# Attention, gated block and Fourier mixing with a channel MLP: the end of the mixing written as an order of jobs

## Chip, cores, metric

The kernel runs on one core of a Trainium2 chip. Times are microseconds of device time; 611.52 us is the median of three runs before (610.66 to 611.62). The engines are named as in the profile: PE is TensorE, DVE VectorE, ACT ScalarE, POOL GpSimd, SP the engine that issues most transfers. PEld is TensorE's loading of weights.

## What is computed

Attention under a mask of hashed buckets (2 batches, 8 heads, 768 positions, 64 per head), a gated block and then, on `x` of 2 x 768 x 512, the part that the change touches:

```python
def _moe2_ref(x, w_ch1, w_ch2) -> np.ndarray:
    X = np.fft.fft(x, axis=1)
    X = np.fft.fft(X, axis=2)
    mixed = np.real(X).astype(np.float32)
    u = x + mixed
    mu = np.mean(u, axis=-1, keepdims=True)
    var = np.mean((u - mu) ** 2, axis=-1, keepdims=True)
    un = (u - mu) / np.sqrt(var + 1e-06)
    ch = np.maximum(un @ w_ch1, 0.0) @ w_ch2
    return (u + ch).astype(np.float32)
```

## The kernel before

The order of all instructions is the order in which the program writes them; there is no scheduler. Each engine works through its own part of that order, and waits when an input or a tile isn't there yet.

**Mixing** (`mixing`). The Fourier transform is done by tables. The output of the gated block comes in 12 parts: batch, even or odd half, and row block `kt` of 128. For each part `own` (L1286) makes 12 matmuls; `fold` copies the result to `y` (ACT) and folds its columns (DVE, L1299); `turn` transposes the fold (PE, L1306), takes the high half on ACT (L1311) and the low half `ft` on DVE (L1312); `along_d` multiplies by the table along the columns (PE, L1321) and splits into `ah` and `al` (ACT L1326 or L1331, DVE L1327 or L1332). Odd parts with `kt` 0 have two folds, so a batch has seven alongs. `mixed` (L1350) transforms along the positions, `total` (DVE, L1356 to L1361) and `both` (POOL, L1371) add it up to `u`.

**Normalising.** For each pair of row blocks (t and t + 3 of six): `stats` (DVE, L1105 and L1106), `root` (ACT, L1110), `scale` (DVE, L1115 and L1116: `rstd` and `shift`), `normal` (ACT, L1120: `un`), `u_transpose` (PE, L1127) and `u_parts` (`bh` on ACT, L1134, `bl` on DVE, L1135).

**Channel MLP** (`channel`). Weights come as 64-bit numbers and are taken apart by `from64`: six steps s0 to s5 on DVE (L221, L229, L230, L234, L235, L243) and ACT (L225, L249). `first` (PE, L1625) multiplies `bh` and `bl` by a block of the first weights, `relu_high` (ACT) and `relu_low` (DVE, L1617) make `hid`, `second` (PE, L1676) multiplies that by the second weights into six accumulators, `flush` (DVE) adds them to `u`. Four blocks of batch 0 are done in this plain way. From then on 13 steps use seven products of sums of weights and tokens instead of eight; the sums (`combos`, DVE, L1501 to L1509) are made ahead, the snapshots (L1747 and L1750) and low halves after a product.

**What sets the order.** In the mixing a loop over `i` from 0 to 13 writes own, alongs, turns and fold of successive parts, with the normalising of batch 0 and the conversion of weight block 3 (`channel_steps(3)`, one or two of its steps for each `i` from 8 on) behind them; after the loop the mixing products of batch 1. In the channel stage `follow` reads 16 strings, `ORDERS`, in which each word is a job of several instructions: `I0a` is the first channel product of weight block 0 for the first half of the rows, `h0a` and `l0a` its relu halves, `S00` a second product, `c51` a step of a weight conversion.

Of the kernel before, what the change touches and what calls it, by code (L numbers as in the profile page):

```python
# [76 lines left out]
""",
    """
M1 A3 A5 A6 M2 A4 s0 F0 c11 F1 B0 h11 B2 B1 M6 l11 M5 B3 s1 B5 B6 F2 B4 s3 F3 W0 M7 W1 M3 F4 c22 W2 c12 F5 A0+
h12 M4 W3 h22 A1+ G0 l12 h21 G1 l22 l21 G2 A3+ G3 A5+ A2+ G4 G5 A4+ A6+  # L80
""",
    """
M1 B0 B2 B1 M2 s0 B3 F0 B5 B6 c11 F1 f0 h11 M6 f1 l11 M5 s1 B4 A0+ F2 s3 A2+ A1+ F3 f2 M7 f3 M3 c22 A3+ F4 A5+
A6+ c12 F5 f4 h12 M4 h22 f5 G0 l12 h21 l22 G1 l21 G2 B0+ A4+ B1+ G3 B2+ G4 G5 B3+
""",
    """
M1 B5 B6 B4 M2 W0 s0 F0 c11 F1 W1 h11 M6 l11 W2 M5 A0+ A2+ s1 F2 s3 W3 F3 A1+ M7 A3+ M3 A5+ c22 A4+ F4 c12 F5
B0+ h12 M4 B2+ h22 B1+ G0 l12 h21 l22 G1 l21 G2 B3+ G3 B5+ B4+ G4 G5
""",
    """  # L90
M1 M2 s0 F0 c11 F1 h11 f0 M6 l11 f1 M5 s1 F2 s3 F3 f2 M7 f3 M3 c22 F4 c12 F5 h12 f4 h22 M4 l12 f5 G0 h21 l22
G1 l21 G2 G3 G4 G5
""",
    """
M1 M2 s0 F0 c11 F1 h11 M6 l11 M5 s1 F2 s3 F3 M7 M3 c22 F4 c12 F5 h12 h22 M4 l12 l22 G0 h21 G1 l21 G2 G3 G4 G5
""",
    """
M1 M2 s0 F0 c11 F1 h11 f0 M6 l11 f1 M5 s1 F2 s3 F3 f2 M7 f3 M3 c22 F4 c12 F5 h12 f4 h22 M4 l12 f5 G0 h21 l22
G1 l21 G2 G3 G4 G5
# [73 lines left out]
def block_kernel(  # L173
# [24 lines left out]
    def from64(words_of, raw, dst, half=False, parts=P, spare=False):  # L198
# [28 lines left out]
        def s2():  # L227
            g = word("g")
            nc.vector.tensor_scalar(g, hi, 0x1FF, 15, op0=ALU.bitwise_and, op1=ALU.logical_shift_left)  # L229
            nc.vector.scalar_tensor_tensor(g, lo, 17, g, op0=ALU.logical_shift_right, op1=ALU.bitwise_or)  # L230

        def s3():
            a, e = word("a"), word("e")
            nc.vector.scalar_tensor_tensor(a, hi, -(2 ** 31), a, op0=ALU.bitwise_and, op1=ALU.bitwise_or)  # L234
            nc.vector.tensor_scalar(e, a, -(2 ** 23), None, op0=ALU.bitwise_and)  # L235
# [15 lines left out]
        return [s0, s1, s2, s3, s4, s5]  # L251
# [773 lines left out]
    rstd, wst, wraw, wnext = [], [], {}, []  # L1025
# [13 lines left out]
    def late_tiles():  # L1039
# [14 lines left out]
        wst.append(pool(ctx, "wst", 2, side="right"))  # L1054
# [29 lines left out]
    def channel_steps(k, spare=False, load=True):  # L1084

        if k >= 2 * NF:
            return [lambda: None] * 6
        i, f = ORDER[k]
        w = w2[f % 4] if i else w1[f % 5]
        st = []  # L1090

        def step(q):
            if not st:
                st.extend(from64(channel_words, wraw[k], lambda: w, spare=spare))
            st[q]()
            if q == 3 and load:
                channel_load(k + 2)

        return [lambda q=q: step(q) for q in range(6)] + [lambda: channel_load(k + 2)] * (not load)

    def stats(b, kt):

        for t in (kt, kt + 3):
            st = wst[0].tile([P, 6], F32, tag="st", name="st")
            nc.vector.bn_stats(st, u[b][:, t, :])  # L1105
            nc.vector.bn_aggr(mu[b][:, t, :], st)  # L1106
# [11 lines left out]
    def normal(b, kt):  # L1118
        for t in (kt, kt + 3):
            nc.scalar.activation(  # L1120
                un[b, t], u[b][:, t, :], AF.Identity, bias=rstd[1][:, b, t : t + 1], scale=rstd[0][:, b, t : t + 1]
            )
# [7 lines left out]
    def u_parts(t, pu):  # L1130
        ts_ = slice(t % 3 * P, (t % 3 + 1) * P)
        pv_ = pu.rearrange("p (c t) -> p c t", c=NC)
        hi, lo = bh[0, t // 3][:, :, ts_], bl[0, t // 3][:, :, ts_]
        nc.scalar.copy(hi, pv_)  # L1134
        nc.vector.tensor_tensor(lo, pv_, f32(hi), op=ALU.subtract)  # L1135

    def mixing(es):
        nonlocal pp
# [155 lines left out]
        def fold(b, s, kt, yp):  # L1294
            y = ys[b, s, kt] = m2.tile([P, DM], F32, tag="y", name="y", bufs=7)
            nc.scalar.copy(y, yp)
            for part in (s,) if s == 0 or kt else (0, 1):
# [18 lines left out]
        def along_d(b, s, kt, part):  # L1316
            fh, fl = turned[b, s, kt, part]
            ops = [(x[:, i, :], tab[:, part, w, i, :]) for x, w in ((fh, 0), (fh, 1), (fl, 0)) for i in range(2)]
            pa = psum()
            for n, (x, w) in enumerate(ops):  # L1320
                nc.tensor.matmul(pa[:, :NL], x, w, start=n == 0, stop=n == len(ops) - 1)  # L1321
            ah, al = sums[b]
            slot = kt if part == s else 3
            high, low = ah[:, part, slot, :], al[:, part, slot, :]
            if part:
                nc.scalar.copy(high, pa[:, :NL])  # L1326
                nc.vector.tensor_tensor(low, pa[:, :NL], f32(high), op=ALU.subtract)  # L1327
            else:

# [56 lines left out]
        for i in range(len(jobs) + 2):  # L1386
# [47 lines left out]
            elif i > 10:  # L1434
                if i == 11:
                    root(0, 2)
# [390 lines left out]
```

## Time and profile before

| | |
|---|---|
| median of the runs | 611.52 us |
| the profiled execution | 613.5 us |
| its span | 611.7 us |
| TensorE busy | 595.0 us, 97% of the span |
| VectorE busy | 537.4 us, 88% |
| ScalarE busy | 378.3 us, 62% |
| GpSimd busy | 228.9 us, 37% |
| mean granted clock of TensorE | 0.994 |

TensorE is busy nearly all the time, so the table alone says little on where time could be lost. The attention ends near 255 us, the gated block and the mixing reach to about 352, and the channel MLP fills the rest. The page's slices of the span show one dip of TensorE's clock, in the slice that begins at 336.

### The profile page before, as it was taken

What the parts mean: (1) busy time and instruction counts of PE and PEld (TensorE: products, weight loads), DVE (VectorE), ACT (ScalarE), POOL (GpSimd) and SP (SyncE); (2) the same over time, 40 slices, a digit from 0 to 9 for tenths busy, and PEclk for the clock granted to TensorE, in tenths of its full rate; (3) what the DMA queues carried; (4) which work ended last, traced back from release to release, by engine and by line L of the source; (5) the groups of instructions that cost most, each with busy time, mean ns of one, the idle gap of its engine ahead of it and who ended that gap; (6) DMA issues with size and microseconds to landing.
All of it is one profiled execution on the core that took longest, in us unless ns stands there. A gap on an engine that the chain in (4) does not pass through costs nothing.

```text
span 611.7 us, 10422 instructions
## 1 busy us (share of the span) xinstructions
PE 595.0 (97%) x3633; PEld 544.6 (89%) x3633; DVE 537.4 (88%) x1041; ACT 378.3 (62%) x747; POOL 228.9 (37%) x272
## 2 busy tenths in 40 slices
PE   8999999999999999999998899999999999999997
PEld 6889999999899989998897899988998899998886
DVE  5999999999899999799789799999999999996345
ACT  5998899998899887863626566344344443442221
POOL 7251488886888898793350230000000000000000
PEclk9999999999999999999999799999999999999999
DMA  5957585856665750162012112021222323220014
GB/s 136 216 134 162 144 189 146 186 147 147 163 163 145 199 134 16 40 238 98 5 65 61 43 35 70 1 70 45 93 70 70 103 70 103 70 71 0 1 40 167
DMA packets 54958, 62.03 MB, mean 101 GB/s; under 512 B 29184, under 2 KB 42664, under 8 KB 54650
## 3 DMA queue, kind: packets, MB, share of 16 engines
q1 hardware_dynamic: 54170, 57.81, 35.7%
q0 software_dynamic: 432, 3.55, 1.5%
q8 instruction: 29, 0.48, 0.3%
q14 instruction: 23, 0.19, 0.1%
q10 hardware_dynamic: 304, 0.01, 0.0%
HBM read 36.74 MB, written 3.19 MB: 65 GB/s over the span
## 4 chain that ended last, share of the span: by engine, by line
PE 68%; DVE 18%; DMA 4%; ACT 3%; issue 2%; SPq 2%; POOL 2%; POOLq 0%; DVEq 0%; ACTq 0%
PE acc L1676 20%; PE pf L1635 14%; PE sp L638 6%; PE op L697 6%; PE ptp L674 5%; DVE sd L649 4%; DVE ptl L686 4%; PE pf L1625 3%; PE ps L302 3%; PE ps L1286 3%; DMA qk<-ht 3%; PE ps L1350 2%; PE late L302 1%; DMA xs<-xc 1%; PE early L302 1%
## 5 line engine op out<-in xcount | busy, mean ns | idle before, releaser
L649 DVE TENSOR_SCALAR_CACHE_REDUCE sd<-sp 128x768 f32<-128x768 f32 x96 | 91.2, 951 | 7.8 <-PE sp L638 7.5
L686 DVE TENSOR_TENSOR ptl<-ptp,pth 128x768 fp32r<-128x768 f32 x96 | 91.5, 954 | 5.5 <-ACT pth L682 3.8
L638 PE MATMUL sp<-qk 128*128 128x512 f32 (+1 forms) x384 | 91.4, 360 | 4.4 <-DVE sd L649 3.0
L656 ACT ACTIVATE sd<-sd,nm 128x768 f32<-128x768 f32 x96 | 90.2, 939 | 1.5 <-DVE sd L649 1.5
L682 ACT CAST pth<-ptp 128x768 fp32r<-128x768 f32 x96 | 77.1, 803 | 18.0 <-PE ptp L774 9.1
L674 PE MATMUL ptp<-ident,sd 128*128 128x128 f32 x576 | 78.5, 272 | 0.2 <-ACT sd L656 0.2
L697 PE MATMUL op<-pth,v 128*128 128x256 f32 x288 | 74.0, 283 | 1.3 <-ACT xc L710 1.3
L697 PE MATMUL op<-ptl,v 128*128 128x256 f32 x288 | 73.8, 286 | 0.0
L638 PEld LDWEIGHTS sp<-qk 128*128 128x128 f32 x384 | 58.2, 189 | 14.1 <-DVE sd L649 7.2
L674 PEld LDWEIGHTS ptp<-ident,sd 128*128 128x128 f32 x576 | 65.8, 140 | 1.1 <-ACT sd L656 0.5
L1676 PE MATMUL acc<-vh,hid 128*128 128x512 f32 x192 | 64.0, 391 | 0.0
L697 PEld LDWEIGHTS op<-pth,v 128*128 128x128 f32 x288 | 54.2, 188 | 6.3 <-ACT xc L710 2.3
L715 POOL TENSOR_TENSOR xm<-xc,xs 64x256 f32<-64x256 f32 x48 | 35.2, 734 | 56.7 <-DMA xs<-xc 39.5
L697 PEld LDWEIGHTS op<-ptl,v 128*128 128x128 f32 x288 | 54.2, 188 | 0.2
L321 POOL TENSOR_TENSOR g<-g,conv_tmp 128x768 f32<-128x768 f32 x27 | 46.7, 1728 | 1.2
L1635 PE MATMUL pf<-t,s 128*128 128x384 f32 x234 | 45.1, 335 | 0.0
L1635 PEld LDWEIGHTS pf<-t,s 128*128 128x128 f32 x234 | 41.3, 188 | 2.7 <-DVE snap L1750 0.3
L1676 PEld LDWEIGHTS acc<-vh,hid 128*128 128x128 f32 x192 | 36.0, 188 | 6.8
L1613 ACT ACTIVATE hid<-snap 128x384 fp32r<-128x384 f32 x39 | 19.6, 521 | 33.3 <-DVE snap L1750 30.2
L1750 DVE TENSOR_TENSOR snap<-snap,pf 128x384 f32<-128x384 f32 x39 | 21.1, 549 | 20.0 <-PE pf L1635 19.9
L225 ACT ACTIVATE cv<-cv,col 128x512 int32<-128x512 int32 x32 | 23.1, 722 | 24.6 <-DVE cv L221 24.4
L1676 PE MATMUL acc<-vl,hid 128*128 128x512 f32 x96 | 37.7, 393 | 0.0
(305 smaller groups left out, 1378.6 us busy)
## 6 DMA issues: line engine op xcount, KB each, us to landing
raw<-in_moe_w_ch_dram SPq DMA_DIRECT2D x32, 512.0 KB
qk<-ht SPq DMA_DIRECT2D x60, 192.0 KB
qk<-lt SPq DMA_DIRECT2D x30, 192.0 KB
rqk<-in_q_dram SPq DMA_DIRECT2D x16, 192.0 KB
rqk<-in_k_dram SPq DMA_DIRECT2D x16, 192.0 KB
rv<-in_v_dram SPq DMA_DIRECT2D x8, 384.0 KB
out_dram<-o SPq DMA_DIRECT2D x12, 256.0 KB
xs<-xc SPq DMA_DIRECT2D x47, 64.0 KB
```

What stands on the lines that cost most here:

```text
L302: nc.tensor.matmul(pv_, w[:, ic, c * P : (c + 1) * P], x[:, ic, :], start=n == 0, stop=n == 3 * NC - 1,)
L321: nc.gpsimd.tensor_tensor(dst, dst, tmp, op=ALU.add)
L638: nc.tensor.matmul(sp[:, cs], q2[i][:, m, qi * P : (qi + 1) * P], k2[i][:, m, cs], start=m == order[0], stop=m == order[1])
L649: nc.vector.tensor_scalar(sd[n], sp, CLAMP, None, op0=ALU.min, op1=ALU.min, accum_out=st[p]["nm"][:, n % 12 : n % 12 + 1],)
L656: nc.scalar.activation(sd[n], sd[n], AF.Exp, bias=st[p]["nm"][:, i : i + 1], scale=-1.0, accum_out=st[p]["sums"][:, i : i + 1],)
L674: nc.tensor.transpose(tp[:, r // 3, c0 : c0 + P], sd[n][:, r * P : (r + 1) * P], ident)
L682: nc.scalar.copy(p_parts(n)[0], tp)
L686: nc.vector.tensor_tensor(lo, tp, f32(ho), op=ALU.subtract)
L697: nc.tensor.matmul(po[kb], v3[:, r, c0 : c0 + P], pt[kb][x][:, r, :], start=r == 0 and x == 0, stop=r == R - 1 and x == 1,)
L715: add[kb] = lambda: nc.gpsimd.tensor_tensor(st[p]["xm"][mr, blk * QB : (blk + 1) * QB], xc[mr, :], xs[mr, :], op=ALU.add)
L1635: nc.tensor.matmul(to, a[x][:, c, :], b_[y][:, c, :], start=not more and n == 0, stop=n == 5, skip_group_check=more,)
L1676: nc.tensor.matmul(accs[t], x[:, ts_], w, start=begin and n == 0, stop=ends(m) and n == 2)
```

## The change

1. The end of the mixing, from part 8 of 12 on, is no longer written by the loop. Every single step (an own product, a fold, a turn, its high and low half, an along, a mixing product, a stats operation, a root, a normalisation, a transposition, a step of a weight conversion) is a job, and a new first string of `ORDERS` (17 in all now) names their order.
2. The first channel products of weight blocks 0 and 1 (`I0a` to `I1b`) and their relu halves are among these jobs, and their results stand in PSUM tiles of the mixing.
3. Jobs that held two or more dependent VectorE operations are taken apart: the steps s2 and s3 of `from64`, `bn_stats` and `bn_aggr`, the four operations of `combos`. All the strings are written anew so that such operations have others between them. The tile of the statistics has 4 buffers instead of 2, and the load of a later weight block is a job of its own.

The arithmetic is the same.

```diff
 ORDERS = (
     """
...
+O8 D6a X7a X7b O9 O10 H7a Y8 L7a Y9 st1 H7b A6a E8 L7b B6a E9 D7a Y10 st0 D7b A7a st3 X8a A7b X9a ag0 ag3 O11
+H8a st4 sq0 H9a L8a ag4 ag1 L9a sq1 E10 rs0 B7a no3 st5 D8a no0 B7b D9a ag5 st2 A8a X10a Y11 r0 B8a H10a r3 ag2
...
+I0a P01 st3+ Z12 P11 st1+ I0b h0a c40 l0a c41 st4+ I1a c43 h0b c34 c45 l0b c42 I1b c47 h1a Z02 c46 P12 l1a c48
...
         def s2():
+            nc.vector.tensor_scalar(
+                word("g"), hi, 0x1FF, 15, op0=ALU.bitwise_and, op1=ALU.logical_shift_left
+            )
+
+        def s2_low():
             g = word("g")
-            nc.vector.tensor_scalar(g, hi, 0x1FF, 15, op0=ALU.bitwise_and, op1=ALU.logical_shift_left)
             nc.vector.scalar_tensor_tensor(g, lo, 17, g, op0=ALU.logical_shift_right, op1=ALU.bitwise_or)
...
-        wst.append(pool(ctx, "wst", 2, side="right"))
+        wst.append(pool(ctx, "wst", 4, side="right"))
...
+    def stats(b, t, n):
+
+        if n == 0:
+            st = sts[b, t] = wst[0].tile([P, 6], F32, tag="st", name="st")
             nc.vector.bn_stats(st, u[b][:, t, :])
-            nc.vector.bn_aggr(mu[b][:, t, :], st)
+        else:
+            nc.vector.bn_aggr(mu[b][:, t, :], sts[b, t])
...
-                if i == 10:
-                    scale(0, 0)
-                    normal(0, 0)
-                stats(0, i - 8)
-                run(wnext.pop(0) for _ in range(2 if i == 10 else 1))
...
-            elif i > 10:
-                if i == 11:
-                    root(0, 2)
-                for t in (i - 11, i - 8):
-                    u_parts(t, u_transpose(0, t, psum))
-                if i < 13:
-                    scale(0, i - 10)
-                    normal(0, i - 10)
-                run(wnext.pop(0) for _ in wnext[:1])
...
+        part_tile = lambda b, f, k: psum()
...
+        for k in (3, 4):
+            for n, x in enumerate(channel_steps(k, singly=True)):
+                last[f"c{k}{n}"] = x
+        for f in range(2):
+            last.update(plain_jobs(0, f))
+        follow(0, ORDERS[0])
...
+            return [lambda o=o: nc.vector.tensor_tensor(o[0], o[1], o[2], op=o[3]) for o in ops]
```

In the new string r0 to r5 are the transpositions of the six row blocks, no0 to no5 the normalisations, rs0 to rs2 the scales, c30 to c38 the steps of weight block 3.

**The second scale of batch 0, on VectorE.** Each row is an operation: line, kind, output <- inputs (a number is that of the buffer). `st` and `mu` are statistics, `cv` and `raw` belong to a weight conversion, `shift` is the second result of `scale`. Before:

```order
L1106 BN_AGGR mu_4305<-st 128x2
L229 TENSOR_SCALAR cv<-raw 128x512
L230 SCALAR_TENSOR_TENSOR cv<-raw,cv 128x512
L234 SCALAR_TENSOR_TENSOR cv<-raw,cv 128x512
L235 TENSOR_SCALAR cv<-cv 128x512
L1327 TENSOR_TENSOR a<-ps,a 128x258
L1312 TENSOR_TENSOR ft<-pw,ft 128x256
L1299 TENSOR_TENSOR fold<-ps,y 128x256
L1135 TENSOR_TENSOR bl_4311<-ps,bh_4310 128x4x128
L1135 TENSOR_TENSOR bl_4313<-ps,bh_4312 128x4x128
L1115 RECIPROCAL rstd<-rstd 128x2
L1116 SCALAR_TENSOR_TENSOR shift<-mu_4305,rstd 128x2
```

Now:

```order
L1138 SCALAR_TENSOR_TENSOR shift<-mu_4305,rstd 128x2
L1445 SCALAR_TENSOR_TENSOR a<-ps,y,a 128x258
L1126 BN_STATS st<-u_4303 128x6
L1443 TENSOR_TENSOR a<-ps,a 128x258
L1128 BN_AGGR mu_4305<-st 128x2
L1126 BN_STATS st<-u_4303 128x6
L1445 SCALAR_TENSOR_TENSOR a<-ps,y,a 128x258
L1128 BN_AGGR mu_4305<-st 128x2
L1383 TENSOR_TENSOR fold<-ps,y 128x256
L1411 TENSOR_TENSOR ft<-pw,ft 128x256
L1137 RECIPROCAL rstd<-rstd 128x2
L1138 SCALAR_TENSOR_TENSOR shift<-mu_4305,rstd 128x2
```

The four `cv` operations that stood between the last statistics and the second `shift` are gone from here, and the two `bl` now stand behind it.

**The last alongs and transpositions of `un`, on TensorE.** L1321 (now L1427) is an along, L1306 (L1397) a turn, L1127 (L1148) the transposition of `un`, L1350 (L1463) a mixing product. Before:

```order
L1321 MATMUL ps<-tab,ft 128x258 x6
L1306 MATMUL pw<-ident,fold 128x128 x2
L1127 MATMUL ps<-ident,un 128x128 x8
L1321 MATMUL ps<-tab,ft 128x258 x6
L1306 MATMUL pw<-ident,fold 128x128 x2
L1127 MATMUL ps<-ident,un 128x128 x8
L1321 MATMUL ps<-tab,ft 128x258 x6
L1127 MATMUL ps<-ident,un 128x128 x8
```

Now:

```order
L1427 MATMUL ps<-tab,ft 128x258 x12
L1397 MATMUL pw<-ident,fold 128x128 x2
L1148 MATMUL ps<-ident,un 128x128 x8
L1427 MATMUL ps<-tab,ft 128x258 x6
L1397 MATMUL pw<-ident,fold 128x128 x2
L1148 MATMUL ps<-ident,un 128x128 x8
L1427 MATMUL ps<-tab,ft 128x258 x6
L1148 MATMUL ps<-ident,un 128x128 x4
L1463 MATMUL ps<-a,seq 128x258 x9
L1463 MATMUL ps<-a,odd 128x258 x2
L1148 MATMUL ps<-ident,un 128x128 x4
L1463 MATMUL ps<-a,seq 128x258 x9
```

Two alongs instead of one stand ahead of the first pair of transposed blocks, and the last pair is taken apart with a mixing product of batch 1 between its blocks.

**A combination of sums among a weight conversion, on VectorE.** `x` and `sums` are the sums of tokens and weights, L1501 to L1504 are now L1641. Before:

```order
L230 SCALAR_TENSOR_TENSOR cv<-raw,cv 128x512
L221 TENSOR_SCALAR cv<-raw 128x512
L1501 TENSOR_TENSOR x<-x 128x256
L1502 TENSOR_TENSOR x<-x 128x256
L1503 TENSOR_TENSOR x<-x 128x256
L1504 TENSOR_TENSOR x<-x 128x256
L1597 TENSOR_TENSOR bq<-sums,bq 128x4x128
```

Now:

```order
L1641 TENSOR_TENSOR sums<-sums 128x256
L252 TENSOR_SCALAR cv<-cv 128x512
L1641 TENSOR_TENSOR x<-x 128x256
L260 SCALAR_TENSOR_TENSOR vl_5022<-cv 128x512
L1641 TENSOR_TENSOR x<-x 128x256
L1186 SCALAR_TENSOR_TENSOR hid<-pf,hid 128x384
L1641 TENSOR_TENSOR x<-x 128x256
L239 TENSOR_SCALAR cv<-raw 128x512
L1641 TENSOR_TENSOR sums<-sums 128x256
```

The four `x` operations, each reading the one before, have steps of a conversion and a relu half between them.

## Rows read from the trace of the kernel before

**Rows 1.** Windows: length, busy us (count) of PE PEld DVE ACT POOL, clock, DMA.

```profile
332.00:334.00 2.00, 1.56 (x14) 1.35 (x12) 1.93 (x5) 1.97 (x6) 0.00 (x0) 1.00 0.00 0
334.00:336.00 2.00, 0.83 (x4) 0.50 (x4) 2.00 (x6) 0.32 (x1) 0.00 (x0) 1.00 0.46 106
336.00:338.00 2.00, 0.56 (x4) 0.44 (x4) 1.10 (x4) 1.43 (x3) 0.00 (x0) 0.95 0.44 156
338.00:340.00 2.00, 2.00 (x11) 1.86 (x10) 1.51 (x4) 1.78 (x5) 0.00 (x0) 0.50 0.00 0
340.00:360.00 20.00, 18.77 (x124) 18.48 (x124) 16.84 (x39) 8.33 (x16) 8.09 (x6) 0.88 0.09 27
440.00:460.00 20.00, 20.00 (x101) 18.03 (x101) 19.66 (x40) 9.60 (x17) 0.00 (x0) 1.00 0.25 81
```

**Rows 2.** Timeline, TensorE at the seam; columns: start us, length us, engine, line, operation.

```profile
315.74 2.01 PE L1286 MATMUL ps<-qk,gh 128*128 128x512 f32 x8
...
328.28 2.08 PE L1286 MATMUL ps<-qk,gh 128*128 128x512 f32 x8
...
331.10 0.89 PE L1321 MATMUL ps<-tab,ft 128*128 128x258 f32 x6
...
332.05 1.04 PE L1127 MATMUL ps<-ident,un 128*128 128x128 f32 x8
332.84 0.72 PE L1321 MATMUL ps<-tab,ft 128*128 128x258 f32 x4
334.79 0.50 PE L1321 MATMUL ps<-tab,ft 128*128 128x258 f32 x2 [1.23 <-DVE ft L1312]
...
337.44 1.82 PE L1127 MATMUL ps<-ident,un 128*128 128x128 f32 x8 [1.81 <-ACT un L1120]
338.91 1.64 PE L1321 MATMUL ps<-tab,ft 128*128 128x258 f32 x6
341.78 1.97 PE L1127 MATMUL ps<-ident,un 128*128 128x128 f32 x8 [1.23 <-ACT un L1120]
343.40 1.87 PE L1350 MATMUL ps<-a,seq 128*128 128x258 f32 x9
...
345.35 1.25 PE L1350 MATMUL ps<-a,seq 128*128 128x258 f32 x9
...
351.95 1.55 PE L1625 MATMUL pf<-bh,w 128*128 128x384 f32 x8
...
360.28 1.04 PE L1127 MATMUL pf<-ident,un 128*128 128x128 f32 x8
```

**Rows 3.** Timeline of VectorE, then one row of ScalarE, same columns, same place.

```profile
331.89 0.40 DVE L229 TENSOR_SCALAR cv<-raw 128x512 int32<-128x512 int32 x1
...
333.65 0.43 DVE L235 TENSOR_SCALAR cv<-cv 128x512 int32<-128x512 int32 x1
...
336.37 0.16 DVE L1116 SCALAR_TENSOR_TENSOR shift<-mu,rstd 128x2 f32<-128x2 f32 x1
...
329.51 0.32 ACT L1110 ACTIVATE rstd<-mu,col 128x2 f32<-128x2 f32 x1
```

**Rows 4.** Groups by line and shape, ScalarE, 300 to 346; busy us, mean ns of one.

```profile
L1120 ACT ACTIVATE un<-u,shift,rstd 128x512 f32<-128x512 f32 x6 | 4.6, 806 | 3.8 <-DVE shift L1116 3.8
L1296 ACT COPY y<-ps 128x512 f32<-128x512 f32 x7 | 4.2, 600 | 5.2 <-POOL u L1371 5.2
...
L1134 ACT CAST bh<-ps 128x512 fp32r<-128x512 f32 x6 | 3.4, 590 | 0.2
...
L1331 ACT ACTIVATE a<-ps,y 128x258 fp32r<-128x258 f32 x5 | 2.4, 471 | 2.2 <-PE ps L1321 2.2
```

**Rows 5.** Timeline of VectorE in a combination of token sums; columns as in rows 2.

```profile
383.27 0.43 DVE L1508 TENSOR_TENSOR sums<-sums 128x256 f32<-128x256 f32 x1
383.73 0.42 DVE L1509 TENSOR_TENSOR sums<-sums 128x256 f32<-128x256 f32 x1
384.08 0.42 DVE L1506 TENSOR_TENSOR sums<-sums 128x256 f32<-128x256 f32 x1
```

More of the change, by code (lines that the diff above doesn't have):

```diff
@@ new lines, in u_low, with plain_b, hid @@
+    def u_low(t, pu):
+        hi, lo, src = u_places(t, pu)
+        nc.vector.tensor_tensor(lo, src, f32(hi), op=ALU.subtract)
+    part_tile = k1 = spare_r = None
+    def plain_b(b, j, k):
+        if b == 1 and k == 1:
+            if j == 0:
+                return [spare_r[:, 2 * x : 2 * x + 2, :] for x in range(2)]
+            return [k1[:, x, :].rearrange("p (c t) -> p c t", c=2) for x in range(2)]
+        return [x[b, k][:, 2 * j : 2 * j + 2, :] for x in (bh, bl)]
+    halves = {}
+    def hid(f):
+        f %= 2
+        if f not in halves:
+            x = flat(pp.tile([P, NC, HS], F32R, tag=f"gh{f}", name="hid", bufs=1), 0, 3)
+            halves[f] = x[:, :S], x[:, S:]
+        return halves[f]
@@ new lines, in relu_high, with relu_low, first @@
+    def relu_high(src, f, k):
+        nc.scalar.activation(hid(f)[0][:, k * HS : (k + 1) * HS], src, AF.Relu)
+    def relu_low(src, f, k):
+        hh, hl = (x[:, k * HS : (k + 1) * HS] for x in hid(f))
+        nc.vector.scalar_tensor_tensor(hl, src, 0.0, f32(hh), op0=ALU.max, op1=ALU.subtract)
+    def first(f, k, b=0):
+        w1h, w1l = w1[f % 5]
+        pf = part_tile(b, f, k)[:, :HS]
+        n = 0
+        for w, x in ((w1h, 0), (w1l, 0), (w1h, 1)):
+            for c in range(NC):
+                nc.tensor.matmul(
+                    pf, w[:, c, :], plain_b(b, c // 2, k)[x][:, c % 2, :], start=n == 0, stop=n == 3 * NC - 1
+                )
+                n += 1
+        return pf
@@ new lines, in follow, with plain_jobs @@
+    def follow(i, order):
+        for x in order.split():
+            n = x.strip("+-")
+            jobs[i + x.count("+") - x.count("-")][n]()
+    jobs, pfs = [{}, {}], {}
+    def plain_jobs(b, f):
+        out = {}
+        for k in range(2):
+            n = f"{f}{'ab'[k]}"
+            out["I" + n] = lambda k=k: pfs.__setitem__((b, f, k), first(f, k, b))
+            out["h" + n] = lambda k=k: relu_high(pfs[b, f, k], f, k)
+            out["l" + n] = lambda k=k: relu_low(pfs[b, f, k], f, k)
+        return out
@@ L1379, in mixing @@
         parts_tiles(1, m2)
-        jobs = [(b, s, kt) for b in range(B) for kt in range(3) for s in range(2)]
+        parts = [(b, s, kt) for b in range(B) for kt in range(3) for s in range(2)]
         def spans(job):
@@ L1443, in mixing, with out_jobs, copied, folded @@
-        wnext.extend(channel_steps(4))
-        run(wnext.pop(0) for _ in range(3))
-        both(1, 0)
-        wnext.pop(0)()
-        for kt in range(1, 3):
-            both(1, kt)
+        last, kept = jobs[0], {}
+        def out_jobs(j):
+            b, s, kt = parts[j]
+            def copied():
+                y = ys[b, s, kt] = m2.tile([P, DM], F32, tag="y", name="y", bufs=7)
+                nc.scalar.copy(y, kept[j])
+            def folded():
+                folding(b, s, kt, kept[j])
+            last[f"O{j}"] = lambda: kept.__setitem__(j, own(b, s, kt))
+            last[f"Y{j}"], last[f"E{j}"] = copied, folded
@@ new lines, in mixing @@
+        for kt in range(3):
+            for s in range(2):
+                mixed_jobs(s, kt)
+            for x, y in (("sq", root), ("rs", scale)):
+                for b in range(B):
+                    jobs[b][f"{x}{kt}"] = lambda b=b, kt=kt, y=y: y(b, kt)
+        for t in range(6):
+            last[f"no{t}"] = lambda t=t: normal(0, t)
+            for b in range(B):
+                for n in range(2):
+                    jobs[b][f"{('st', 'ag')[n]}{t}"] = lambda b=b, t=t, n=n: stats(b, t, n)
+            turn_jobs(t)
@@ L1466, in channel @@
             un[1, t] = n0[:, t, :]
-        hid = [flat(pp.tile([P, NC, HS], F32R, tag=f"gh{i}", name="hid", bufs=1), 0, 3) for i in range(2)]
-        hid = [(x[:, :S], x[:, S:]) for x in hid]
         for f in (3, 4):
```

389 lines of the change are left out of this document (192 added, 197 removed).

## The prediction

> **What bounds the kernel now.** The view by windows comes first. In 440 to 460, in the middle of the channel stage, TensorE is busy for all 20.00 us, at full clock, and VectorE for 19.66 [rows 1]. There is nothing to win there unless a matmul goes, and the change takes none away. At the seam between mixing and channel stage it is otherwise: TensorE is busy 1.56, 0.83 and 0.56 us in three neighbouring stretches of 2 us, and then its granted clock is 0.50 [rows 1]. The reader should look for exactly this: a busy share that falls, and the clock after it.
>
> The timeline of TensorE tells who stopped it. 1.23 us before 334.79 it waits for VectorE's `ft` (the low half of a turned fold), 1.81 before 337.44 and 1.23 before 341.78 for ScalarE's `un`, the normalised row block [rows 2]. ScalarE is no more than the messenger there. The square root of the second block is done at 329.51 + 0.32 = 329.83, but VectorE delivers the scale and shift that `un` needs at 336.37 + 0.16 = 336.53 [rows 3]. In between stand four operations of a weight conversion, from 331.89 to 333.65 + 0.43 = 334.08 [rows 3], and the `ft` for which TensorE waits at 334.79 also stands behind them. So the bound at the seam is **the order on VectorE**, not the amount of work there.
>
> **What the seam loses now.** I add up TensorE's work from the first own product of part 8 (315.74) to the end of the first channel products (360.28), 44.54 us [rows 2], as if nothing ever stopped it:
> - 4 own products at 331.10 − 328.28 = 2.82: 11.3
> - 6 alongs with a turn each at 332.05 − 331.10 = 0.95: 5.7; a seventh along, six matmuls
> - 66 mixing matmuls. 55 of them take 351.95 − 345.35 = 6.60, 0.12 each: 7.9; the seventh along has the same shape: 0.7
> - 24 transposes of `un`, eight in 332.84 − 332.05 = 0.79: 2.4
> - 4 first channel products, 360.28 − 351.95: 8.3
>
> That is 36.3; 44.5 − 36.3 = **8.2 us are lost**. Of them 4.3 are the three stops. The half clock costs 2.9: eight transposes 1.82 and 1.97 instead of 1.04, an along 1.64 instead of 0.89, and the first mixing product 345.35 − 343.40 = 1.95 instead of 11 × 0.12 = 1.32 [rows 2]. The rest, about 1, is the emptying and filling around each stop.
>
> **The rewritten end of the mixing.** On VectorE the conversion of weight block 3 goes behind the scales, as the listing of the orders shows, and its operations are spread among others. I walked through the new order by hand, each operation starting when its engine and its inputs are free, with the durations of the rows. My estimates: the first scale is ready near 329.0; from there ScalarE runs without a stop through three `un` (0.81 each), two `bh` (0.59), a `y` (0.60), two `a` (0.47), a turned half (at most 0.47) and a root (0.32) [rows 3, 4]. That is 5.9, less 0.1 of overlap at each of nine seams (two `un` in a row take 1.52 where the mean would give 1.61), 5.1: the second-half `un` of block 1 comes at about 334.1. TensorE has transposed blocks 0 and 3 by then, has done two more alongs, and wants it at 332.8. So **a stop of 1.3 us stays**, and one of about 0.3 behind it for the other `un` of this block. From 334.8 on I find no stop: `r2` and `r5` stand behind an along and a mixing product, by which time their `un` is ready. These 1.6 us include what the filling costs, so the seam gives 8.2 − 1.6 = 6.6; the walk summed start by start gives 7.3. I take **6.9**.
>
> The clock: in 332 to 336 TensorE was busy 1.56 + 0.83 = 2.39 of 4 us, and the granted clock was still 1.00 in both halves; it fell after another 0.56 in 2 us [rows 1]. In the walk the worst 4 us (332 to 336) hold 2.4 us of work and a full stretch follows. I take it that the clock stays up; that it falls is rival B.
>
> **First channel products as jobs of the mixing.** On TensorE they stand behind the last mixing product in both orders, so nothing changes there; they now come in the mixing's PSUM tiles, and the relu halves go in front of the second products' work. Cost 0 on TensorE, hidden by the four products' own 8.3 us: the inputs `bh` and `bl` of all blocks must exist by the first of them, at about 344.6 in the walk, and the last `bl` (w5) is done at about 341. Without that cover it would be about one `bh`/`bl` pair, 1.2 us. The queues of GpSimd and of the DMA issuer hold the same instructions in the same order, but for two neighbouring adds on GpSimd; the load of weight block 5 is issued later in VectorE's sequence, as a job of its own, and used some 15 us after that: 0.
>
> **Dependent operations kept apart.** 135 neighbouring pairs of dependent operations on VectorE become 25 by the two orders. The price of one: 383.73 − 383.27 = 0.46 from start to start where the second reads what the first wrote, 384.08 − 383.73 = 0.35 where it does not [rows 5]. So 0.11 each, and 110 × 0.11 = 12 us of VectorE's time over some 280 us. None of this is on the path by itself, since TensorE is full (20.00 of 20). It is what allows VectorE to keep up when all of the channel stage starts 7 us earlier: VectorE has only 0.34 us to spare in 20 [rows 1]. Value on the path between 0 (as I take it) and a gain of a few tenths where TensorE waits a little for a half.
>
> The Trainium skill, "VectorE: DVE Perf Modes", section "The DRAIN you can't avoid", says that a chain of operations with a semaphore after each takes as long as one with a semaphore only at its end ("the semaphore costs nothing extra here"). By that sentence the second part would gain VectorE nothing. The two gaps of rows 5 speak against it for operations that read each other's output. What follows if it holds is rival C.
>
> **The sum.** Profiled execution 613.5, of which the span is 611.7. 613.5 − 6.9 = 606.6. The profiled execution lies 2.0 above the median of 611.5, so I forecast **604.6 us**. With nothing lost at the seam it is 603.3; the low end, 602.6, allows another 0.7 for the short waits of the later steps that I counted at nothing.
>
> **Rivals.**
> B. *The clock falls anyway*, at the stop of 332.8, and one spell of about 7 us at half clock stays. For: it did fall after the stops of before. Against: full clock in 332 to 336 with the same busy time [rows 1]. Price 2.9, as now: 607.5. Chance 0.10.
> C. *The gain is given back in the channel stage*, since VectorE cannot get ahead. If keeping apart saves nothing, VectorE has to find 6.9 us. It idles 20.00 − 16.84 = 3.16 in 340 to 360 [rows 1], so 3.7 come back as waits of TensorE in the later steps: 608.3. Chance 0.10.
> D. *The new interleaving delays the operation that TensorE waits for*, and the kernel is slower. In each of the 13 steps of seven products, a snapshot's sum or the low half of a relu now has conversion operations ahead of it that it had not. Such an operation takes (333.65 − 331.89) / 3 = 0.59 [rows 3]. One of them on the path in each step costs 13 × 0.59 = 7.6, more than the 6.9: 612.2; two, 620. It decides from 0.53 us a step. For: VectorE is at 19.66 of 20. Against: TensorE showed no waits there at the same load, and the lows of the weights are ready some microseconds ahead in the walk. Chance 0.08.
> E. *It doesn't do what it says*: the stops only move. Whatever starts earlier waits for the last `un`, `a` or stats as before, and the first channel products cannot fill the hole since they stand behind the last mixing product. 611.5. Chance 0.06.
>
> **How the numbers follow.** My forecast has 0.66, B 0.10, C 0.10, D 0.08, E 0.06. The range of 8 in 10 reaches from 602.6 to 608.5: it takes in B and C and leaves out D, E and the tails of the forecast. A measurement of this kernel can tell about 0.2%, 1.2 us, from no change. Faster: forecast, B and C, 0.86. Within 0.2%: E, 0.06. Slower: D, 0.08.
>
> **What would show it.** Right: TensorE's row has one stop of 1 to 1.5 us near 333 and none of over 0.5 after 335; its clock reads 1.0 throughout 330 to 350; the first channel products end near 353 instead of 360.28; and each later step keeps its distance, so that the end of the span moves by the same 7 us. VectorE's second `shift` stands at about 332 instead of 336.37. Gaps from start to start of a `sums` operation fall to 0.35. Wrong in its size: a clock of 0.5 in 334 to 342 (B), or a lead of 7 at 353 that melts towards 540 with short waits for VectorE (C). Wrong in its sign: TensorE under 20.00 of 20 in the channel stage, with `snap` or `hid` of VectorE as the releaser (D).

## The result, and the profile after

The changed kernel takes 604.0 us (median of 4 runs, 603.66 to 605.35) beside 611.4 us for the kernel before (4 runs, 610.66 to 611.62): a ratio of 0.9885, 95% interval 0.9867 to 0.9903. By the ratio that is 7.0 us less (the medians lie 7.4 apart), where 6.9 was the forecast: 604.6 us. The profiled execution has a span of 603.5 us.

The windows at the seam come first; the columns are those of [rows 1].

```profile
330.00:332.00 2.00, 2.00 (x20) 2.00 (x19) 1.74 (x6) 1.87 (x6) 0.00 (x0) 1.00 0.00 0
332.00:334.00 2.00, 1.15 (x10) 0.91 (x10) 1.94 (x7) 2.00 (x4) 0.00 (x0) 1.00 0.00 0
334.00:336.00 2.00, 1.96 (x18) 1.72 (x16) 1.94 (x6) 2.00 (x6) 0.00 (x0) 1.00 0.00 0
336.00:338.00 2.00, 2.00 (x20) 2.00 (x19) 1.56 (x4) 2.00 (x6) 0.00 (x0) 1.00 0.00 0
340.00:360.00 20.00, 20.00 (x123) 18.80 (x122) 19.55 (x48) 8.16 (x16) 8.85 (x6) 1.00 0.19 56
440.00:460.00 20.00, 20.00 (x100) 17.90 (x99) 19.14 (x38) 9.39 (x18) 0.00 (x0) 1.00 0.34 105
```

In 340 to 360 TensorE was busy for 18.77 us at a clock of 0.88 before [rows 1]; now it is 20.00 at 1.00. One stretch of 2 us is left with less than 1.9 of work. ScalarE is the engine that is now full there: 1.87, 2.00, 2.00, 2.00.

The timeline of TensorE at the seam, columns as in [rows 2]:

```profile
315.16 2.01 PE L1366 MATMUL ps<-qk,gh 128*128 128x512 f32 x8
...
332.43 0.38 PE L1397 MATMUL pw<-ident,fold 128*128 128x128 f32 x2
333.66 1.36 PE L1148 MATMUL ps<-ident,un 128*128 128x128 f32 x8 [0.85 <-ACT un L1141]
334.77 0.97 PE L1427 MATMUL ps<-tab,ft 128*128 128x258 f32 x6
...
344.36 1.55 PE L1194 MATMUL ps<-bh,w 128*128 128x384 f32 x8
...
352.68 4.28 PE L1776 MATMUL acc<-w,hid 128*128 128x512 f32 x18
```

The three stops of [rows 2] have become one, of 0.85 us, still for `un`. Inside this row TensorE waits a little once more, for the second `un`: the eight transpositions take 334.77 − 333.66 = 1.11 until the next row begins, where they took 0.79 before. From the first own product of part 8 to the end of the first channel products it is 352.68 − 315.16 = 37.52 us, where it was 44.54: **7.02 us less in this stretch alone**. What follows takes 603.5 − 352.68 = 250.8, and took 611.7 − 360.28 = 251.4. So the lead is held to the end. (The two profiled spans differ by 8.2, more than the medians; 0.58 of it lies ahead of this stretch.) VectorE delivers the two scales here:

```profile
328.20 0.16 DVE L1138 SCALAR_TENSOR_TENSOR shift<-mu,rstd 128x2 f32<-128x2 f32 x1
...
332.03 0.16 DVE L1138 SCALAR_TENSOR_TENSOR shift<-mu,rstd 128x2 f32<-128x2 f32 x1
```

The second one stood at 336.37 [rows 3].

### The profile page after: what moved, and what is told of

Its sections match the earlier page's. It is cut to its first block, busy times and chain, and to the rows that moved or that the text cites. A ratio compares the mean times of both kernels' runs of the same rounds, so it can differ in the third digit from the quotient of the medians.

```text
span 603.5 us, 10420 instructions
## 1 busy us (share of the span) xinstructions
PE 590.6 (98%) x3633; PEld 541.8 (90%) x3633; DVE 529.4 (88%) x1041; ACT 378.1 (63%) x747; POOL 229.9 (38%) x272
## 4 chain that ended last, share of the span: by engine, by line
PE 72%; DVE 8%; POOL 7%; DMA 5%; ACT 2%; issue 2%; SPq 1%; POOLq 0%; DVEq 0%; ACTq 0%
PE acc L1776 22%; PE pf L1735 16%; PE sp L657 5%; PE op L716 5%; PE ps L1366 5%; PE ptp L693 4%; DMA qk<-ht 3%; PE pf L1194 3%; PE ps L321 3%; DVE sd L668 3%; DVE ptl L705 3%; PE ps L1463 2%; DMA xs<-xc 2%; POOL xm L734 2%; PE late L321 1%
## 5 line engine op out<-in xcount | busy, mean ns | idle before, releaser
L1831 ACT COPY snap<-pf 128x384 f32<-128x384 f32 x39 | 18.8, 481 | 36.6 <-PE pf L1735 36.4
L1776 PE MATMUL acc<-gl,hid 128*128 128x512 f32 x144 | 37.7, 395 | 0.0
```

Source lines behind the costliest of these rows:

```text
L1776: nc.tensor.matmul(accs[t], x[:, ts_], w, start=begin and n == 0, stop=ends(m) and n == 2)
```

## Experiments

The runs came in three groups, each with the kernel before run beside it on the same chip (medians 612.2, 613.2 and 614.0 us), so ratios are compared, not times; 0.001 is 0.6 us. The changed kernel stands at 0.9885. In brackets stands the 95% interval of a ratio; where two intervals overlap, the runs alone don't tell the kernels apart.

**Only the seam undone (e_old_seam).** The first string is written in the order of the kernel before; the channel stage stays as changed.

```diff
-O8 D6a X7a X7b O9 O10 H7a Y8 L7a Y9 st1 H7b A6a E8 L7b B6a E9 D7a Y10 st0 D7b A7a st3 X8a A7b X9a ag0 ag3 O11
...
+O10 D8a A8a B8a X9a H9a L9a Y10 E10 sq1 rs0 no0 no3 st2 ag2 st5 ag5 c32 c36 c33 c37 c38
+O11 D9a A9a B9a X10a H10a L10a Y11 E11 sq2 r0 v0 w0 r3 v3 w3 rs1 no1 no4 c34
```

> The changed kernel with only its first string of orders rewritten: the end of the mixing stands again in the order of the kernel before (the conversion of block 3 ahead of the second scale, halves directly behind their products), while all strings of the channel stage stay as changed. Theory (the gain is the order of VectorE at the seam): the stops of 1.2 to 1.8 us and the spell of half clock return, 610 to 612 us. Rival (the gain comes from VectorE's time saved in the channel stage): 604 to 606.

Measured: 613.39 us, ratio 1.0024 (1.0008 to 1.004). TensorE's timeline shows the old stops, and one that is new, behind the first channel products:

```profile
334.08 0.51 PE L1427 MATMUL ps<-tab,ft 128*128 128x258 f32 x2 [1.23 <-DVE ft L1411]
...
336.72 1.62 PE L1148 MATMUL ps<-ident,un 128*128 128x128 f32 x8 [1.81 <-ACT un L1141]
...
340.97 1.97 PE L1148 MATMUL ps<-ident,un 128*128 128x128 f32 x8 [1.27 <-ACT un L1141]
...
361.11 3.69 PE L1776 MATMUL acc<-w,hid 128*128 128x512 f32 x15 [0.47 <-DVE hid L1186]
```

The new strings of the channel stage are worth nothing by themselves, even though VectorE is busy 530.1 us here instead of 537.4. The 1.5 us above the kernel before hold the stop of 0.47, which my way of writing the tail brought in; the rest is not explained.

**The new seam with the old channel stage (e_old_channel).** The reverse. Only the second products ahead of the transpositions of batch 1 stay as changed.

```diff
-I0a W5 A2 W6 tb2- A6 td2- I0b h0a ta1- te2- l0a th2- tb1- td0- F0 td1- h0b te0- F1 te1- th0- f0 F2 l0b th1- F3
...
+I0a W7 th2- I0b tl0- h0a l0a tl1- F0 h0b F1 l0b F2 f0 F3 f1 F4 f2 F5 f3 f4 I1a f5 tl2- I1b h1a A0 A2 A6 A1 l1a G0
```

> The changed seam (first string) with the channel stage in the order of the kernel before: dependent operations side by side, some 70 pairs more than in the changed kernel; only the second products of blocks 0 and the first of block 1 stay ahead of the transpositions of batch 1, as changed. If the keeping apart is worth nothing on the path: 603.5 to 605. If it is what lets VectorE follow 7 us earlier (70 x 0.11 = 7.7 us more work against about 5 us of slack): waits of TensorE for snap, hid or the weight sums after 380, and 606 to 609.

Measured: 610.57 us, ratio 0.9956 (0.9941 to 0.997). The seam has its one stop of 0.85, but 4.3 us (0.0071) of the gain are given back behind it. TensorE's timeline and a window from there:

```profile
368.66 1.12 PE L1147 MATMUL pf<-ident,un 128*128 128x128 f32 x8 [0.86 <-DVE hid L1185]
...
399.36 0.97 PE L1734 MATMUL pf<-t,s 128*128 128x384 f32 x4 [0.70 <-ACT snap L1830]
...
401.19 1.32 PE L1734 MATMUL pf<-t,s 128*128 128x384 f32 x6 [0.50 <-DVE snap L1833]
...
404.36 1.33 PE L1734 MATMUL pf<-t,s 128*128 128x384 f32 x6 [0.46 <-ACT snap L1830]
```

```profile
400.00:420.00 20.00, 19.04 (x94) 16.62 (x93) 19.55 (x40) 9.07 (x16) 0.00 (x0) 1.00 0.15 48
```

TensorE is at 19.04 of 20 with VectorE at 19.55. From 420 on hardly a stop is left (19.97 and then 20.00 of 20): TensorE is then as late as VectorE needs it to be. This is rival C, seen in a kernel in which its condition holds. With e_old_seam it makes a square: the seam alone gives 0.9956, the new strings of the channel stage alone 1.0024, both 0.9885. The second is worth something only where the first has been done. That it is the keeping apart which counts in these strings is not shown by the square, since everything in them was written anew; the next two runs bear on that.

**Dependent pairs put side by side again (e_adjacent), and apart again at the same late place (e_near).** A part of one string of each (the others are edited alike):

```diff
 e_adjacent against the changed kernel
-M1 T4 A5- A8- A7- M2 T5 s0 A4- T6 B0- F0 c11 B1- F1 B2- W0 h11 M6 B6- B3- M5 s1 l11 B5- B8- B7- F2 s3 T7 F3 M7
+M1 A8- A3- A7- A5- M2 T2 T3 T4 T5 s0 A4- T6 B0- F0 c11 B1- F1 W0 h11 M6 B2- B6- M5 s1 l11 B8- B3- B7- B5- F2 s3 T7
...
 e_near against e_adjacent
-G0 h21 U0+ G1 l21 G2 G3 W2 W3 W4 W5 W6 G4 A0 A2 A6 G5 A1 W7
+W2 l22 G0 h21 W3 U0+ G1 W4 l21 G2 G3 W5 W6 G4 A0 A2 A6 G5 A1 W7
```

> The changed kernel with its seam untouched; in the strings of the channel stage some 80 dependent pairs (the halves of conversion steps 2 and 3, the four operations of each combination) are put side by side again, the earlier one moved down to the later. By the rows, 80 x 0.11 = 9 us more of VectorE's time, of which it has about 0.55 in 20 to spare, 5 us from 350 to 540: if that decides, 3 to 5 us come back, 607 to 609. If the keeping apart is worth nothing (the rule of the semaphore that costs nothing, or enough slack): 603.5 to 604.7, and the distances of dependent operations from start to start remain 0.35.

> The kernel of e_adjacent, in which the earlier operation of a dependent pair was moved down to the later one, with one or more other VectorE operations put back between about 60 of the 80 pairs; everything stays as late as in e_adjacent, give or take an operation. If side-by-side pairs were what cost 11 us there: 60 x 0.11 = 6 to 7 us of VectorE's time come back, 607 to 610. If it was the lateness of the moved operations (one set of word buffers, so the next conversion starts later): 613 to 616.

Measured: e_adjacent 615.63 us, ratio 1.0053 (1.0034 to 1.0073); e_near 605.21 us, ratio 0.989 (0.9865 to 0.9915). In the first 10.3 us come back (0.0168), more than the whole gain and far more than the 3 to 5 that were expected; the second is better than expected. By the traces some 70 pairs stand side by side in e_adjacent and not in e_near, 39 of combinations and 30 of conversions. Keeping them apart is worth 0.0163, 10 us, and lateness alone costs nothing that the runs show: e_near is as fast as the changed kernel. The busy times of the engines (e_adjacent, then e_near):

```profile
PE 595.1 (97%) x3633; PEld 540.4 (88%) x3633; DVE 535.5 (87%) x1041; ACT 376.2 (61%) x747; POOL 229.7 (37%) x272
```

```profile
PE 590.5 (98%) x3633; PEld 541.6 (90%) x3633; DVE 529.5 (88%) x1041; ACT 376.9 (63%) x747; POOL 229.8 (38%) x272
```

VectorE is busy 6.0 us longer for some 70 pairs, 0.09 each; with the 0.03 for which it idles in front of a dependent operation (383.73 − 383.27 − 0.43 in [rows 5]) that is close to the 0.11 of [rows 5]. The timeline of VectorE shows it operation by operation: four combinations one behind the other in e_adjacent, 1.79 from the first start to the last end; and in e_near, with one other operation in each gap.

```profile
409.00 1.79 DVE L1642 TENSOR_TENSOR x<-x 128x256 f32<-128x256 f32 x4
```

```profile
392.22 0.42 DVE L1641 TENSOR_TENSOR x<-x 128x256 f32<-128x256 f32 x1
392.56 0.42 DVE L252 TENSOR_SCALAR cv<-cv 128x512 int32<-128x512 int32 x1
392.89 0.42 DVE L1641 TENSOR_TENSOR x<-x 128x256 f32<-128x256 f32 x1
393.23 0.69 DVE L260 SCALAR_TENSOR_TENSOR wl<-cv 128x512 fp32r<-128x512 int32 x1
```

From start to start 0.34, 0.33 and 0.34 there; (1.79 − 0.42) / 3 = 0.46 in the chain. The 10 us are more than the 6.0: a lengthened chain puts off `snap` and `hid`, and TensorE stops for them, longest ahead of 399.38 (1.22 us), 446.14 (0.72), 497.06 (0.89) and 499.01 (0.62), each time with the emptying of its own. That this makes up the other 4 us is an argument; no run separates it. By the Trainium skill, "VectorE: DVE Perf Modes", section "The DRAIN you can't avoid", eight copies with a semaphore after each take as long as eight with one only at the end. For operations that read each other's output the trace doesn't agree: 0.46 against 0.34 from start to start, and 10 us in the kernel.

**The conversion ahead of the second scale again (e_conv_ahead: all four operations; e_half_conv: two).** The two steps before them, c30 and c31, go further ahead; e_conv_ahead:

```diff
-E11 A9a sq2 L10a D10a v0 rs1 B9a v3 X11a w0 no4 w3 no1 r4 rs2 c30 H11a r1 c32 no2 L11a D11a c36 A10a r2 v1 B10a
+E11 A9a sq2 L10a D10a v0 c32 c36 c33 c37 rs1 B9a v3 X11a w0 no4 w3 no1 r4 rs2 H11a r1 no2 L11a D11a A10a r2 v1 B10a
```

> The changed kernel with the four operations of weight block 3's conversion (steps 2 and 3) put back directly ahead of the second scale, as in the kernel before; everything else of the new order stays. They take 2.2 us. If this is what set the stop: the stop of 0.85 us before the second pair of transpositions grows to about 3, with TensorE at full clock 606.2; if the clock falls in this stop too, 608 to 609. If it isn't on the path: 604.

> As e_conv_ahead, with only two of the four conversion operations (step 2) ahead of the second scale, 1.1 us. The stop before the second pair of transpositions grows from 0.85 to between 1.5 and 2. If the clock stays up in such a stop: 604.7 to 605.2. If it falls as it did with the stop of 2.41: 606 to 607.

Measured: e_conv_ahead 608.67 us, ratio 0.9928 (0.9903 to 0.9953); e_half_conv 605.42 us, ratio 0.9878 (0.9847 to 0.991). The windows of the first, then of the second:

```profile
332.00:334.00 2.00, 1.48 (x13) 1.24 (x11) 1.97 (x5) 1.56 (x5) 0.00 (x0) 1.00 0.00 0
334.00:336.00 2.00, 0.11 (x1) 0.11 (x2) 1.93 (x7) 0.98 (x2) 0.00 (x0) 0.85 0.19 27
336.00:338.00 2.00, 2.00 (x10) 2.00 (x11) 1.18 (x4) 1.97 (x5) 0.00 (x0) 0.50 0.69 236
338.00:340.00 2.00, 2.00 (x16) 2.00 (x15) 1.60 (x3) 1.38 (x3) 0.00 (x0) 0.79 0.00 0
```

```profile
332.00:334.00 2.00, 1.59 (x15) 1.35 (x12) 1.93 (x7) 1.68 (x5) 0.00 (x0) 1.00 0.00 0
334.00:336.00 2.00, 1.01 (x7) 0.77 (x8) 1.92 (x7) 1.90 (x4) 0.00 (x0) 1.00 0.00 0
336.00:338.00 2.00, 2.00 (x19) 2.00 (x18) 1.22 (x3) 2.00 (x5) 0.00 (x0) 1.00 0.00 0
```

With four operations the stop is 2.41 us, TensorE was busy 1.59 of 4 us, and the clock falls to 0.50. With two the stop is 1.35, it was busy 2.60 of 4, and the clock stays at 1.00. The first costs 0.0043, 2.6 us: 1.56 of longer stop, and about 1, the remainder, for the clock. The second costs 0.5 us by its stop, too little for the runs to show.

**The first transposition of batch 1 ahead of the second products (e_tr_first).** This I had not priced: the changed string of the channel stage lets seven second products of blocks 0 and 1 go in front of it.

```diff
-S00 S02 S03 ag3 S04 ag0 ag4 st5 sq0 S01 rs0 st2 no0 S05 ag1 c50 no3 S10 ag5 c52 tr0 W0+ c51 ur0 c56 sq1 S11 tc0
+ag3 ag0 ag4 st5 sq0 rs0 st2 no0 ag1 c50 no3 tr0 S00 S02 S03 S04 S01 S05 S10 ag5 c52 W0+ c51 ur0 c56 sq1 S11 tc0
```

> The changed kernel with one TensorE step moved: the first transposition of batch 1 (tr0) stands ahead of the second products again, as in the kernel before, and the statistics that it needs with it. In the changed kernel TensorE ends the first channel products at 352.7 and the un that tr0 reads ends at 355.37 + 1.52 = 356.9. If the place of tr0 is a part of the gain: a stop of about 4 us near 353, with half clock behind it, 608 to 611. If the un simply comes earlier: 604.

Measured: 609.46 us, ratio 0.9946 (0.9919 to 0.9972), 3.7 us (0.0061) more than the changed kernel. TensorE's timeline behind the first channel products:

```profile
354.30 1.12 PE L1148 MATMUL pf<-ident,un 128*128 128x128 f32 x4 [3.39 <-ACT un L1141]
355.07 6.67 PE L1776 MATMUL acc<-w,hid 128*128 128x512 f32 x18
```

The stop of 3.39 is there, and the 18 matmuls behind it take 6.67 us at a granted clock of 0.50 where they take 4.28 in the changed kernel. So more than half of the seam's gain would have met this wait: batch 1's `un` comes no earlier for it.

**The first channel products back in the channel stage (e_first_back).**

```diff
-        for f in range(2):
-            last.update(plain_jobs(0, f))
         follow(0, ORDERS[0])
...
-            if f > 1:
-                jobs[1].update(plain_jobs(0, f))
+            jobs[1].update(plain_jobs(0, f))
...
-            return tile_f()
+            return tile_a(2 + k) if f == 1 and b == 0 else tile_f()
```

> The changed kernel with its second part undone: the first channel products of blocks 0 and 1 and their relu halves are jobs of the channel stage again, in the PSUM tiles of the channel stage, written behind all conversions and totals of the mixing; on TensorE they stand in the same place. If this part is worth nothing, as I put it: within 0.7 us of the changed kernel. If the relu halves, now behind four totals and a conversion on VectorE, are what the second products wait for: a stop of 1 to 3 us near 353 and 605.5 to 608.

Measured: 607.15 us, ratio 0.9911 (0.9882 to 0.994). The intervals of this and of the changed kernel overlap, so the runs alone don't show a cost. But TensorE's timeline shows two stops that the changed kernel doesn't have, 1.7 us together:

```profile
348.74 1.65 PE L1194 MATMUL acc<-bh,gl 128*128 128x384 f32 x8 [0.87 <-DVE y L1471]
...
354.71 3.71 PE L1774 MATMUL acc<-w,hid 128*128 128x512 f32 x15 [0.85 <-DVE hid L1186]
```

The first is for a total of the mixing, behind which the accumulator becomes free, the second for a relu half that stands behind totals and a conversion. The difference of the ratios, 0.0026, is 1.6 us.

**The smallest edit of the kernel before (e_before_scale).** Scale and normalisation ahead of the transposed halves, and the conversion of block 3 pushed behind, among the mixing products. With it the conversion of block 4 comes later too, behind the second of these products.

```diff
+                if i < 13:
+                    scale(0, i - 10)
+                    normal(0, i - 10)
                 for t in (i - 11, i - 8):
                     u_parts(t, u_transpose(0, t, psum))
-                if i < 13:
-                    scale(0, i - 10)
-                    normal(0, i - 10)
...
+        wnext.extend(channel_steps(3))
+        run(wnext.pop(0) for _ in range(2))
         both(1, 0)
+        run(wnext.pop(0) for _ in range(4))
```

> The kernel before with two edits at the seam and nothing else: the conversion of weight block 3 comes after the scales, among the mixing products, and the scale and normalisation of a pair of blocks stand ahead of the transposed halves of the pair before it. The channel stage keeps its dependent operations side by side. Theory (order on VectorE at the seam, kept by a full TensorE): most of the gain, 605 to 607.5. Rival C (VectorE cannot get ahead without the keeping apart): the seam becomes shorter, but later steps wait for VectorE, 608.5 to 611, with TensorE under 20.00 of 20 us after 360.

Measured: 616.74 us, ratio 1.0067 (1.0044 to 1.0091), slower than either expectation. Its stops at the seam are shorter (0.61, 0.94, 0.18 and 0.61 us), and the stretch from the first own product of part 8 to the end of the first channel products is 2.0 us shorter: 361.52 − 4.09 − 314.88 = 42.55 instead of 44.54. But the clock fell at the seam all the same, and another stop came. Rows of VectorE, of GpSimd, and of TensorE:

```profile
345.52 1.67 DVE L230 SCALAR_TENSOR_TENSOR cv<-raw,cv 128x512 int32<-128x512 int32 x1
347.12 1.78 DVE L234 SCALAR_TENSOR_TENSOR cv<-raw,cv 128x512 int32<-128x512 int32 x1
...
345.30 3.05 POOL L1371 TENSOR_TENSOR u<-y 128x512 f32<-128x512 f32 x2 [25.89 <-DVE y L1361]
...
361.52 2.34 PE L1127 MATMUL pf<-ident,un 128*128 128x128 f32 x8 [4.09 <-ACT un L1120]
```

The conversion operations now run beside GpSimd's adds of `u` and take 1.67 and 1.78 us, where the first three operations of a conversion took 333.65 − 331.89 = 1.76 together in [rows 3]. The totals stand behind them on VectorE, so the `un` of batch 1 is late, and TensorE waits for it: the wait of e_tr_first, larger. How much of the 4.09 is the place of the operations, and how much their slowness beside the adds, no run separates. Moving the conversion away was not enough; where it goes matters as much.

**ScalarE: `un` ahead of `bh` (e_un_first),** an attempt on the last stop.

```diff
-E11 A9a sq2 L10a D10a v0 rs1 B9a v3 X11a w0 no4 w3 no1 r4 rs2 c30 H11a r1 c32 no2 L11a D11a c36 A10a r2 v1 B10a
+E11 A9a sq2 L10a D10a rs1 B9a X11a no4 no1 v0 v3 w0 w3 r4 rs2 c30 H11a r1 c32 no2 L11a D11a c36 A10a r2 v1 B10a
```

> The changed kernel, in which ScalarE makes the un of blocks 4 and 1 (no4, no1) ahead of the bh of blocks 0 and 3 (v0, v3) instead of behind them. The scale is ready at 332.19 in the changed kernel and the un begins at 332.76, so the stop of 0.85 us on TensorE should fall to about 0.3: 0.5 us less than the changed kernel, if nothing else is late (the bh and bl are wanted 10 us later). Rival: the PSUM tiles of blocks 0 and 3 come free later and TensorE waits for these instead: no gain or up to 0.5 us slower.

Measured: 607.88 us, ratio 0.9906 (0.9876 to 0.9936), no gain. TensorE's timeline:

```profile
333.84 1.36 PE L1148 MATMUL ps<-ident,un 128*128 128x128 f32 x8 [0.28 <-ACT un L1141]
...
335.77 0.74 PE L1427 MATMUL ps<-tab,ft 128*128 128x258 f32 x4 [0.57 <-ACT ft L1406]
...
337.61 0.51 PE L1427 MATMUL ps<-tab,ft 128*128 128x258 f32 x2 [1.10 <-DVE ft L1411]
```

And VectorE's:

```profile
334.99 1.29 DVE L1161 TENSOR_TENSOR bl<-ps,bh 128x512 fp32r<-128x512 f32 x2 [1.72 <-ACT bh L1157]
```

The stop for `un` fell from 0.85 to 0.28 as expected, and the last `ft`, high and low half, came 1.67 us too late instead: the stretch to the end of the first channel products is 355.08 − 315.91 = 39.17 us here, 1.65 longer than in the changed kernel. It wasn't the PSUM tiles. ScalarE now idles for 0.29 us until the scale is there, a time that `bh` filled before, so the high half of `ft` behind it comes later. And VectorE idles for 1.72 us until `bh` is there, because in its own order the two `bl` stand ahead of the low half of `ft`. So one engine's order was changed and the other's left. Whether `un` first pays when VectorE's order follows is not tested. None of the versions that were run beats the changed kernel by more than the noise.

## Why the prediction was right, and where it was not

**What bounded the kernel: the order at the seam, shown; the order on VectorE, shown in part.** Putting the whole seam back takes the whole gain away (e_old_seam), but that puts the order of every engine back. Putting only the conversion of block 3 back ahead of the second scale, its four operations on VectorE and what leads up to them, brings a stop of 2.41 us and the half clock, 2.6 of the 7 us (e_conv_ahead). How the rest is shared among the other moves, the two `bl` behind the scale and the second along ahead of the transpositions among them, no run separates.

**The sum over the seam: right to 0.1 us, partly by luck.** 6.9 was forecast and 7.02 measured in that stretch. By the prediction's own sum of TensorE's work, 36.3, now 37.52 − 36.3 = 1.2 us are lost, where the walk left 1.6: the stop of 0.85, for which it had 1.3, and 1.11 − 0.79 = 0.3 inside the transpositions, the short second wait that it had put at 0.3. The scales came a little earlier or as the walk put them: the first at 328.36 for 329.0, the second at 332.19 for 332. So the mechanism held term by term. But 6.9 was chosen between two sums, 6.6 and 7.3, and a hit to 0.1 is closer than these allowed. And the four differences listed for the half clock add up to 3.1, not 2.9; the emptying and filling around the stops is then 0.8.

**The clock: right that it stayed up, the reason not shown.** It reads 1.00 from 330 to 360. A stop 1.56 us longer than the 0.85 brought it down (e_conv_ahead), one 0.5 us longer did not (e_half_conv). But the comparison of the prediction, how long TensorE was busy in 4 us, would have failed elsewhere. In e_un_first it was busy 1.38 + 0.90 = 2.28 of 4 us, less than the 2.39 of [rows 1], and the clock stayed up. In e_before_scale it was busy 1.26 + 1.25 = 2.51 of 4 us, more than that, no stop there was longer than 0.94, and the clock fell to 0.50. The windows of e_un_first, then of e_before_scale:

```profile
334.00:336.00 2.00, 1.38 (x10) 0.91 (x9) 1.01 (x2) 1.72 (x4) 0.00 (x0) 1.00 0.00 0
336.00:338.00 2.00, 0.90 (x7) 0.70 (x7) 1.97 (x7) 1.41 (x3) 0.00 (x0) 1.00 0.00 0
338.00:340.00 2.00, 2.00 (x19) 2.00 (x18) 1.72 (x5) 2.00 (x5) 0.00 (x0) 1.00 0.00 0
```

```profile
334.00:336.00 2.00, 1.26 (x8) 0.79 (x8) 0.90 (x2) 2.00 (x5) 0.00 (x0) 1.00 0.00 0
336.00:338.00 2.00, 1.25 (x6) 0.83 (x6) 1.35 (x5) 0.77 (x2) 0.00 (x0) 1.00 0.00 0
338.00:340.00 2.00, 1.66 (x10) 1.42 (x11) 0.56 (x1) 2.00 (x5) 0.00 (x0) 0.80 0.00 0
340.00:342.00 2.00, 2.00 (x11) 2.00 (x11) 2.00 (x5) 1.14 (x3) 0.00 (x0) 0.50 0.00 0
```

There, four stops of at most 0.94 brought it down, where e_conv_ahead had one of 2.41. So the clock stayed up as forecast, but the reason given for it does not carry over to these two runs; how near rival B was is open.

**Keeping apart: right that it lets VectorE follow, wrong in its price on the path.** I wrote 0 to a few tenths. With the seam as changed, the new strings are worth 4.3 us (e_old_channel against the changed kernel), and without that 0 (e_old_seam); pushing the pairs together inside the new strings costs 10 (e_adjacent against e_near). I had this number in the text, as the price of rival C (3.7 given back), but under the term itself I looked at the kernel before, in which TensorE is full and VectorE has as much time as it needs. The price per pair, 0.11 from start to start, was right: 0.46 − 0.34 = 0.12 measured. Of it some 0.09 is busy time; the busy time of the changed kernel's VectorE fell by 537.4 − 529.4 = 8.0 us, not by the whole 12.

**First channel products: mis-sized.** I put 0. The profile of e_first_back has 1.7 us of stops for it, though the runs alone can't tell it from nothing. The step that failed is that I priced their place on TensorE alone: their PSUM tiles and the place of their relu halves on VectorE changed as well.

**A term that was missing.** That seven second products now go ahead of the first transposition of batch 1 is 3.7 us by e_tr_first. My walk had it in, since it followed the new order, but the text doesn't name it, and a reader would have thought the seam's gain safe without it.

**Rivals.** B, C, D and E did not come true. C's mechanism exists and was kept off by the new strings of the channel stage. Of D there is no trace in the changed kernel: TensorE is at 20.00 of 20 in each window from 360 to 580. e_adjacent shows, for another reason, what such stops for `snap` and `hid` cost: 10 us.

## To carry to other kernels

When the engine that bounds a kernel is full nearly everywhere, look for the short stretch in which its busy share falls, and there for the engine whose order, not load, makes it wait. Before counting the gain, ask who must now run earlier by that much: VectorE had 0.3 us to spare in 20 where TensorE is full, and with the old strings of the channel stage 4.3 of the 7 us were given back. And price a part of a change with the other parts in place as well as without them: the same edit was worth nothing alone and 4.3 us beside the other.

## What the runs showed of the hardware

Operations on VectorE that read the output of the one directly before them start 0.46 us apart where independent ones of the same size start 0.34 apart; over a kernel this was 0.09 us of busy time a pair, and 10 us on the path for some 70 pairs (e_adjacent against e_near).

Beside GpSimd's adds, VectorE's conversion operations L230 and L234 took 1.67 and 1.78 us (e_before_scale); the same operations took 0.69 each in the kernel before where no add ran. Its totals, which read one operand from PSUM, kept 0.40 to 0.42 beside the same adds in the changed kernel (one row of the kernel before, then VectorE and GpSimd in the changed kernel):

```profile
332.32 0.69 DVE L230 SCALAR_TENSOR_TENSOR cv<-raw,cv 128x512 int32<-128x512 int32 x1
...
341.41 0.42 DVE L1469 TENSOR_TENSOR y<-y,ps 128x257 f32<-128x257 f32 x1
...
341.04 5.54 POOL L1488 TENSOR_TENSOR u<-y 128x512 f32<-128x512 f32 x4 [21.35 <-DVE y L1474]
```

The Trainium skill, "SBUF — State Buffer", section "Who interferes with whom", says that VectorE and GpSimd contend for one pair of ports, and that a VectorE instruction with at most one SBUF input outside the two-port modes doesn't contend. The trace agrees: 0.42 for the totals, and 1.67 for a conversion step with two SBUF inputs.
